# A soft threshold as a relu on ScalarE and one two-step operation on VectorE, in place of a clip and a subtraction on VectorE

## The chip, the cores and the metric

The kernel runs on one core of a Trainium2 chip. The metric is the device time of one execution in microseconds (us), taken as the median of several runs. A core has five engines that work side by side, each through its own instructions in order: TensorE (PE; its weight loads are listed apart as PEld), VectorE (DVE), ScalarE (ACT), GpSimd (POOL) and SyncE (SP), which here issues most of the DMAs. They wait for one another by semaphores.

## The reference: a filter in frequency space, then a gated feed-forward layer

Eight sequences of 3008 rows and 256 channels go through a real Fourier transform along the rows, a complex 256 by 256 product with a bias, a **soft threshold** of the real and of the imaginary part, and the inverse transform. The 24064 rows that come out go through a feed-forward layer with a gate.

```python
X = np.fft.rfft(x, axis=1)
Yr = Xr @ w_r - Xi @ w_i + b_r
Yi = Xr @ w_i + Xi @ w_r + b_i
lam = 0.01
Yr = np.sign(Yr) * np.maximum(np.abs(Yr) - lam, 0.0)
Yi = np.sign(Yi) * np.maximum(np.abs(Yi) - lam, 0.0)
y = np.fft.irfft(Yr + 1j * Yi, n=x.shape[1], axis=1)
...
gate = 1.0 / (1.0 + np.exp(-(x @ w_gate)))
return gate * (x @ w_val) @ w_out
```

The soft threshold draws a value towards zero by 0.01, and values between -0.01 and 0.01 become zero.

## The kernel before

**The transform.** 3008 = 64 x 47, so each transform is two small matrix products with a pass through HBM between them. Stage A (`product_a`, line 186) multiplies along 47, and its result goes to HBM as `zd`. Stage B works for one sequence in 12 steps of `q`, each with two of 24 frequency classes: `fwd_b` multiplies `zf`, read from `zd`, with a table (matmul `pb`, line 247) and splits the result into a rounded high part `xsh` and a rest `xsl` (ScalarE at lines 260 and 264, VectorE at 262 and 265); `mix` is the complex product (matmuls `pm` and `pm3`, line 282), the bias (`yt`, line 284) and the sums `ys` (lines 288 and 289). Then comes `soft`, the soft threshold, from `ys` to `yc`, a tile of 128 partitions by 512 numbers. `mix` splits `yc` into `yh` (ScalarE, line 293) and `yl` (VectorE, line 294), and `inv_b` multiplies these with the inverse table (matmuls `pi`, lines 319 to 321); ScalarE copies the result out of PSUM (`vz`, line 323), and it goes to HBM as `vd`. `inv_a` reads it as `vf` and does the last product (matmul `pia`, line 351), whose result is kept as `yth` and `ytl` or written out as `yf`.

**The feed-forward layer.** The first 9 chunks of 512 rows go through `ffn1` and `ffn2`: matmuls `pg` and `pv` (lines 410 to 412, three for each pair of high and low parts), the sigmoid `sg` (line 416), the product with `pv` (line 418), its split into `hh` and `hl` (lines 426 and 427) and the second product `po` (lines 438 to 440). The rest goes through another form of the same layer, `half`, which holds no soft threshold.

**What sets the order.** The first sequence alone is done in an order written out by hand: steps `q` with `fwd_b(q)`, `mix4(q - 1)` and `inv_b(q - 2)`. `mix4` (line 304 for the matmuls, 306 for the bias) is a form of `mix` that calls `soft` too and hands `yc` on unsplit (line 316). Beside it the weights are unpacked from 64-bit words (`ops`, lines 796 to 804; the relu at 797 takes its bias from the column `ebias`). The other seven sequences run beside the feed-forward chunks. There the loops only give the order of the program, and a scheduler with costs of its own places the instructions on each engine. So a changed operation can move its neighbours. `half` and the last part are again in an order by hand.

**PSUM.** Three banks are shared by `pb`, `pm`, `pm3`, `pi`, `pia` and stage A's `pa` (`FFT_BANKS`), three by `pg` and `pv`, two by `po`. A matmul into a bank waits until ScalarE or VectorE has read what was in it. Each engine takes its instructions in order, so what stands behind a waiting instruction waits as well.

`soft` is called 96 times: 12 times in `mix4` and 84 times in `mix`. The column `ebias` is one of the 128 columns of a tile of which the rest is not used.

Of the kernel before, what the change touches and what calls it, by code (L numbers as in the profile page):

```python
# [9 lines left out]
F32 = mybir.dt.float32  # L10
# [3 lines left out]
AF = mybir.ActivationFunctionType  # L14
ALU = mybir.AluOpType
# [7 lines left out]
LAM = float(np.float32(0.01))  # L23
# [86 lines left out]
def tile_fft_mix_ffn(ctx: ExitStack, tc, x, w_r, w_i, b_r, b_i, w_one, w_out, mf, mi, mis, fa, fb, out):  # L110
    nc = tc.nc

    B, D, S = x.shape[0], w_r.shape[0], R1 * R2
    P = 128
# [12 lines left out]
    sub = nc.vector.tensor_sub  # L127
# [9 lines left out]
    cw = fft.enter_context(tc.tile_pool(name="cw", bufs=1))  # L137
# [8 lines left out]
    def f2k(name):  # L146
        return p2.tile([P, 2, D], F32, tag="f2k", bufs=NF2K, name=name)
# [120 lines left out]

    def soft(s):
        c = f2k("yc")  # L270
        nc.vector.tensor_scalar(c, s, -LAM, LAM, op0=ALU.max, op1=ALU.min)
        sub(c, s, c)
        return c

    def mix(b, q):
        xh, xl = held.pop(("xs", b, q))
        pm = bank("pm")
        p3 = bank("pm3")[:, :D]
        for part, w, o in ((2, 0, pm[:, :D]), (0, 1, pm[:, D:]), (1, 2, p3)):
            mms = [(a[:, ct, part], w_sb[:, ct, v, w]) for ct in range(CT) for a, v in ((xh, 0), (xh, 1), (xl, 0))]  # L280
            for i, (l, r) in enumerate(mms):
                nc.tensor.matmul(o, l, r, start=(i == 0), stop=(i == len(mms) - 1))  # L282
        t = f2k("yt")
        nc.vector.tensor_add(t, pm.rearrange("p (a d) -> p a d", a=2), bias_sb)
        s = f2k("ys")
        for i in range(2):
            rows = slice(64 * i, 64 * i + 64)
            nc.vector.tensor_add(s[0:64, i], p3[rows], t[rows, 0])
            nc.vector.tensor_add(s[64:128, i], t[rows, 0], t[rows, 1])
        c = soft(s)  # L290
        yh = r2k("yh")
        yl = r2k("yl")
        nc.scalar.copy(yh, c)
        sub(yl, c, yh)
        held["ys", b, q] = yh, yl

    def mix4(b, q):
        xh, xl = held.pop(("xs", b, q))
        pm = bank("pm").rearrange("p (q d) -> p q d", q=2)
        for i in range(2):  # L300
            mms = [(a[:, ct, i, at:at + P], w[:, ct, v]) for ct in range(CT)
                   for w, at in ((w_sb[:, :, :, 0], 64), (wi_sb, 0)) for a, v in ((xh, 0), (xh, 1), (xl, 0))]
            for k, (l, r) in enumerate(mms):
                nc.tensor.matmul(pm[:, i], l, r, start=(k == 0), stop=(k == len(mms) - 1))
        s = f2k("ys")
        nc.vector.tensor_add(s, pm, bias4.rearrange("p (o d) -> p o d", o=1).broadcast_to([P, 2, D]))
        held["ys", b, q] = soft(s)
# [444 lines left out]

    bias_sb = cw.tile([P, 2, D], F32, name="bias_sb")
    bias4 = p0.tile([P, D], F32, name="bias4")
    ebias = cw.tile([P, P], F32, name="ebias")[:, :1]
    fb_sb = const.tile([2 * NQ, P], F32, name="fb_sb")
    w1h = const.tile([P, NF, 2, CT, P], F32R, name="w1h")
    w1l = const.tile([P, NF, 2, CT, P], F32R, name="w1l")
# [94 lines left out]
    ffn, own0, u0 = ffn_units()  # L853
    na = R1 // 8
    nc.vector.memset(ebias, -896.0 * 2.0 ** 23)
    mfs, mis_ = {}, {}
    beside = [(b, h) for b in groups[2] for h in range(R1 // 4)]
    waiting = list(beside)
# [142 lines left out]
    for j in range(NF, len(ffn)):  # L1001
        c, f = divmod(j, NF)
# [39 lines left out]
    a, b, c, d = banks[0]  # L1042
# [62 lines left out]
```

## Time and profile before

| | us |
|---|---|
| median of 3 runs | 2779.26 (2777.61 to 2780.85) |
| the profiled execution | 2779.58 |
| its span, from the first instruction's start to the last one's end | 2777.7 |
| TensorE's granted clock over the span | 0.999 of full speed |

The profile's page gives the busy time of each engine, the chain of work that ended last, and the groups of instructions by line, with the mean duration of one and the idle time ahead of them. In the names, `yc<-ys` is an instruction that writes tile `yc` and reads `ys`; `L272` is line 272. The trace can also be asked for the busy time by stretch of time, for a table of who waited for whom, and for a timeline, which gives each instruction's start and length in us, and in brackets how long its engine stood idle before it and what ended that.

### The profile page before, as it was taken

Reading aid. Unit: us, or ns where it says so; the run is one execution under the profiler, and the core shown is the slowest. Engines: PE = TensorE matmul, PEld = TensorE weight load, DVE = VectorE, ACT = ScalarE, POOL = GpSimd, SP = SyncE. Lnnn points to the kernel's source line nnn. Section 1 sums busy time; section 2 is a strip of 40 time slices with the busy share of each in tenths; the row PEclk is TensorE's granted clock in tenths of the full one; section 3 lists DMA queues with packets and bytes.
Section 4 is the critical chain, followed back from the end, with each engine's and each line's share of the span. In section 5 each row is a group of like instructions: output and inputs, shape, how many; then the busy total and the mean of one; then the engine's idle time right before and its main releaser. Section 6 shows DMA issues by size and latency. Waiting matters only on the chain.

```text
span 2777.7 us, 38257 instructions
## 1 busy us (share of the span) xinstructions
PE 2760.4 (99%) x13896; PEld 2305.2 (83%) x13896; DVE 2080.6 (75%) x3109; ACT 1307.4 (47%) x2276; POOL 709.4 (26%) x638
## 2 busy tenths in 40 slices
PE   9999999999999999999999999999999999999999
PEld 6778888888899988888888888888888888888887
DVE  5778778767787636777777777777777777777776
ACT  4665554555455444444444444444444444444443
POOL 0211010223200001333333343333333333333321
PEclk9999999999999999999999999999999999999999
DMA  9867545665554561000000000000000000000000
GB/s 293 266 214 198 171 139 157 193 190 184 178 156 147 168 196 58 31 16 16 31 31 16 16 31 31 31 11 21 31 31 16 16 31 31 27 4 31 31 16 16
DMA packets 173469, 241.01 MB, mean 87 GB/s; under 512 B 14592, under 2 KB 124896, under 8 KB 173280
## 3 DMA queue, kind: packets, MB, share of 16 engines
q1 hardware_dynamic: 163776, 214.93, 25.0%
q0 software_dynamic: 9408, 23.60, 2.6%
q8 instruction: 110, 1.80, 0.3%
q14 instruction: 79, 0.65, 0.1%
q10 hardware_dynamic: 96, 0.04, 0.0%
HBM read 134.17 MB, written 104.33 MB: 86 GB/s over the span
## 4 chain that ended last, share of the span: by engine, by line
PE 95%; DVE 3%; DMA 1%; ACT 1%; issue 0%; SPq 0%; DVEq 0%; ACTq 0%
PE pd L670 11%; PE pc L670 11%; PE pa L670 11%; PE po L646 7%; PE po L645 7%; PE po L647 7%; PE pb L670 6%; PE pm L282 5%; PE pia L351 4%; PE pa L186 3%; PE pb L247 3%; PE pg L410 2%; PE pg L411 2%; PE pg L412 2%; PE pv L410 2%; PE pv L412 2%
## 5 line engine op out<-in xcount | busy, mean ns | idle before, releaser
L647 PE MATMUL po<-hl,w 128*128 128x512 f32 x912 | 354.8, 389 | 0.0
L645 PE MATMUL po<-hh,w 128*128 128x512 f32 x912 | 354.8, 389 | 0.0
L646 PE MATMUL po<-hh,w 128*128 128x512 f32 x912 | 354.8, 389 | 0.0
L729 POOL TENSOR_TENSOR c<-c,c 128x512 f32<-128x512 f32 x114 | 147.7, 1296 | 801.2 <-DVE c L725 588.1
L670 PE MATMUL pc<-s,w1h 128*128 128x512 f32 x912 | 280.8, 389 | 0.0
L670 PE MATMUL pa<-a,w1h 128*128 128x512 f32 x912 | 280.8, 389 | 0.0
L725 DVE TENSOR_TENSOR c<-u,pc 128x512 f32<-128x512 f32 x228 | 156.5, 687 | 91.5 <-PE pc L670 85.6
L700 DVE TENSOR_TENSOR u<-u,pb 128x512 f32<-128x512 f32 x228 | 155.2, 681 | 90.7 <-PE pb L670 61.1
L617 ACT CAST hh<-v 128x512 fp32r<-128x512 f32 x114 | 70.7, 620 | 306.1 <-DVE v L710 306.1
L645 PEld LDWEIGHTS po<-hh,w 128*128 128x128 f32 x912 | 171.2, 188 | 35.6
L670 PEld LDWEIGHTS pc<-s,w1h 128*128 128x128 f32 x912 | 171.2, 188 | 35.5
L670 PEld LDWEIGHTS pa<-a,w1h 128*128 128x128 f32 x912 | 171.2, 188 | 35.5
L647 PEld LDWEIGHTS po<-hl,w 128*128 128x128 f32 x912 | 171.2, 188 | 35.5
L646 PEld LDWEIGHTS po<-hh,w 128*128 128x128 f32 x912 | 171.2, 188 | 35.5
L621 POOL TENSOR_TENSOR hl<-c,hh 128x512 fp32r<-128x512 f32 x114 | 152.3, 1336 | 186.0 <-ACT hh L617 186.0
L282 PE MATMUL pm<-w_sb,xsh 128*128 128x256 f32 x1008 | 188.5, 286 | 1.6 <-ACT xf L187 1.1
L670 PE MATMUL pc<-s,w1l 128*128 128x512 f32 x456 | 177.4, 389 | 0.0
L670 PE MATMUL pa<-a,w1l 128*128 128x512 f32 x456 | 177.4, 389 | 0.0
L702 DVE TENSOR_TENSOR v<-u,pc 128x512 f32<-128x512 f32 x228 | 156.9, 688 | 24.5 <-DVE u L700 0.9
L731 DVE TENSOR_TENSOR u<-u,pd 128x512 f32<-128x512 f32 x228 | 156.6, 687 | 24.5 <-DVE c L725 0.9
L704 DVE TENSOR_TENSOR v<-v,pd 128x512 f32<-128x512 f32 x228 | 156.7, 687 | 24.0 <-DVE v L702 0.5
L696 ACT COPY u<-pa 128x512 f32<-128x512 f32 x228 | 133.7, 586 | 69.4 <-PE pa L670 69.2
(174 smaller groups left out, 6721.1 us busy)
## 6 DMA issues: line engine op xcount, KB each, us to landing
zf<-zd SPq DMA_DIRECT2D x96, 256.0 KB, 3.6
vf<-vd SPq DMA_DIRECT2D x128, 192.0 KB, 3.0
out_dram<-ot SPq DMA_DIRECT2D x93, 256.0 KB, 2.2
vd<-vz SPq DMA_DIRECT2D x84, 256.0 KB, 2.8
ypair<-yd SPq DMA_DIRECT2D x19, 1024.0 KB, 4.9
yd<-yf SPq DMA_DIRECT2D x103, 188.0 KB, 2.9
xf<-in_x_dram SPq DMA_DIRECT2D x48, 384.0 KB, 4.1
zd<-xf SPq DMA_DIRECT2D x44, 384.0 KB, 3.3
```

What stands on the lines that cost most here:

```text
L282: nc.tensor.matmul(o, l, r, start=(i == 0), stop=(i == len(mms) - 1))
L621: sub_(hl, h, hh)
L645: nc.tensor.matmul(o, wh, hh, start=(f == 0), stop=False)
L646: nc.tensor.matmul(o, wl, hh, start=False, stop=False)
L647: nc.tensor.matmul(o, wh, hl, start=False, stop=(f == NF - 1))
L670: nc.tensor.matmul(o, l, r, start=not more and l is wh and r is xh, stop=l is wl, skip_group_check=more)
L700: add(u, u, b)
L702: add(v, u, c)
L704: add(v, v, d)
L725: add(c12, u, c)
L729: nc.gpsimd.tensor_mul(c12, g12, c12)
L731: add(u, u, d)
```

## The change

In `soft`, the clip to the band from -0.01 to 0.01 and the subtraction of the clipped value give way to two other operations. With s the input and LAM = 0.01, ScalarE computes c = relu(s - LAM), and VectorE then computes min(s + LAM, c) in one operation of two steps. Above the band that is s - LAM, below it s + LAM, and zero within. ScalarE's activation takes its bias from a tile, so a second column of the tile of `ebias` is filled with -LAM.

```diff
     def soft(s):
         c = f2k("yc")
-        nc.vector.tensor_scalar(c, s, -LAM, LAM, op0=ALU.max, op1=ALU.min)
-        sub(c, s, c)
+        nc.scalar.activation(c, s, AF.Relu, bias=lam_sb)
+        nc.vector.scalar_tensor_tensor(c, s, LAM, c, op0=ALU.add, op1=ALU.min)
         return c
...
-    ebias = cw.tile([P, P], F32, name="ebias")[:, :1]
+    both = cw.tile([P, P], F32, name="ebias")
+    ebias, lam_sb = both[:, :1], both[:, 1:2]
...
     nc.vector.memset(ebias, -896.0 * 2.0 ** 23)
+    nc.vector.memset(lam_sb, -LAM)
```

Lines 271 and 272 keep their numbers: 271 is now ScalarE's relu and 272 VectorE's two-step operation. Lines behind 755 move on by one, those behind 857 by two.

**Place 1, the first sequence, in the order by hand.** ScalarE's queue in one step of `q`: the end of a weight's unpacking (`w_107`, `raw`), then the copy `vz` out of PSUM and the parts `xsh` and `xsl` of the next step. Before:

```order
L803 CAST w_107<-raw_297 128x2x256
L800 ACTIVATE raw_408<-raw_408 128x512
L323 COPY vz<-pi 128x512
L253 CAST xsh<-pb 128x4x128
L256 ACTIVATE xsh<-xsh 128x4x64
L256 ACTIVATE xsl<-xsl 128x4x64
```

And with the change:

```order
L804 CAST w_107<-raw_298 128x2x256
L801 ACTIVATE raw_409<-raw_409 128x512
L271 ACTIVATE yc<-ys,ebias 128x512
L323 COPY vz<-pi 128x512
L253 CAST xsh<-pb 128x4x128
L256 ACTIVATE xsh<-xsh 128x4x64
L256 ACTIVATE xsl<-xsl 128x4x64
```

The relu, which waits for `ys` from VectorE, stands ahead of `vz`, `xsh` and `xsl`. (Its bias is listed under the name of the tile, `ebias`.) Nothing else moves; on VectorE one operation stands where two stood.

**Place 2, the fourth soft threshold of the second sequence, where the scheduler sets the order.** VectorE's queue before, with the last two sums into `ys` first, then the sum `xsf` and the rest `xsl` for the next step, the rest `yl`, and the next step's `yt`:

```order
L288 TENSOR_TENSOR ys<-pm_2138,yt 64x256
L289 TENSOR_TENSOR ys<-yt 64x256
L262 TENSOR_TENSOR xsf<-xsf 128x2x128
L271 TENSOR_SCALAR yc<-ys 128x512
L272 TENSOR_TENSOR yc<-ys,yc 128x512
L265 TENSOR_TENSOR xsl<-xsf,xsh 128x768
L294 TENSOR_TENSOR yl<-yc,yh 128x512
L284 TENSOR_TENSOR yt<-pm,bias_sb 128x512
```

And with the change:

```order
L288 TENSOR_TENSOR ys<-pm_2139,yt 64x256
L289 TENSOR_TENSOR ys<-yt 64x256
L262 TENSOR_TENSOR xsf<-xsf 128x2x128
L284 TENSOR_TENSOR yt<-pm,bias_sb 128x512
L272 SCALAR_TENSOR_TENSOR yc<-ys,yc 128x512
L265 TENSOR_TENSOR xsl<-xsf,xsh 128x768
L294 TENSOR_TENSOR yl<-yc,yh 128x512
```

The next step's `yt` has moved ahead of the threshold. TensorE's queue at the same place, matmuls of `pg` and `pv` around the first ones that read `yh` and `yl`, before:

```order
L412 MATMUL pg<-yth,w1l 128x512
L319 MATMUL pi<-yh,mi_sb 128x256
L410 MATMUL pg<-yth,w1h 128x512
L411 MATMUL pg<-ytl,w1h 128x512
L412 MATMUL pg<-yth,w1l 128x512
L410 MATMUL pv<-yth,w1h 128x512
L320 MATMUL pi<-yl,mi_sb 128x256
```

And with the change:

```order
L412 MATMUL pg<-yth,w1l 128x512
L410 MATMUL pg<-yth,w1h 128x512
L411 MATMUL pg<-ytl,w1h 128x512
L412 MATMUL pg<-yth,w1l 128x512
L410 MATMUL pv<-yth,w1h 128x512
L319 MATMUL pi<-yh,mi_sb 128x256
L411 MATMUL pv<-ytl,w1h 128x512
L412 MATMUL pv<-yth,w1l 128x512
L410 MATMUL pv<-yth,w1h 128x512
L320 MATMUL pi<-yl,mi_sb 128x256
```

L319, which reads `yh`, now stands behind four more matmuls. Over the whole program TensorE's instructions are the same, and their order differs at a score of places like this one. In 72 of the 96 units of the change, VectorE's two-step operation stands directly behind the last sum into `ys`; in the other 24, one or two operations of another step lie between. SP's loads and stores change places with a neighbour at about thirty places.

## The prediction

> **What bounds the kernel now.** I read the page first, for the shares and the chain of work that ended last.
>
> ```profile
> span 2777.7 us, 38257 instructions
> PE 2760.4 (99%) x13896; PEld 2305.2 (83%) x13896; DVE 2080.6 (75%) x3109; ACT 1307.4 (47%) x2276; POOL 709.4 (26%) x638
> PE 95%; DVE 3%; DMA 1%; ACT 1%; issue 0%; SPq 0%; DVEq 0%; ACTq 0%
> ```
>
> TensorE is busy for 2760.4 of 2777.7 us and holds 95% of the chain. All its idle time together is 17.3 us. Next the table by stage says where the touched lines lie: the soft threshold runs 12 times between 35 and 95 us and 84 times between 190 and 950 us, and nowhere else.
>
> ```profile
> 35.00:95.00 60.00, 56.62 (x419) 52.83 (x418) 48.83 (x86) 34.63 (x66) 8.96 (x13) 0.97 0.90 277
> 190.00:430.00 240.00, 237.66 (x1463) 202.17 (x1462) 191.41 (x342) 122.22 (x204) 28.80 (x42) 1.00 0.57 168
> 430.00:690.00 260.00, 259.20 (x1601) 220.69 (x1600) 189.46 (x321) 131.22 (x225) 52.35 (x82) 1.00 0.60 183
> 690.00:950.00 260.00, 258.82 (x1775) 236.91 (x1774) 202.29 (x356) 130.38 (x224) 19.62 (x29) 1.00 0.51 153
> 1065.00:2778.00 1713.00, 1708.51 (x7537) 1414.44 (x7535) 1336.23 (x1825) 770.50 (x1345) 571.57 (x426) 1.00 0.07 23
> ```
>
> The columns are the stretch, then the busy time of TensorE, weight loads, VectorE, ScalarE and GpSimd. From 190 to 950 us TensorE is busy for 237.66 + 259.20 + 258.82 = 755.7 of 760 us: 4.3 us idle. VectorE is busy for 583 us (77%), ScalarE for 384 (50%). The 1713 us behind 1065 hold no soft threshold. The change does not touch a matmul, so it can act only through the waits of TensorE. These are they, from the tables of who waited for whom between 190 and 950 us (us in total, times, longest):
>
> ```profile
> PEld pa L186 <- ACT vz L323: 7.2, 11, 0.7
> PEld pia L351 <- DVE ys L288: 4.9, 5, 1.4
> PEld pi L319 <- ACT yh L293: 2.4, 5, 0.7
> PEld pa L186 <- ACT yf L367: 1.5, 5, 0.3
> PEld pa L186 <- ACT hh L426: 1.1, 4, 0.3
> PEld pi L320 <- DVE yl L294: 0.2, 1, 0.2
> PE pi L319 <- ACT yh L293: 0.6, 2, 0.3
> ```
>
> PEld is the weight load, which runs ahead of the matmul, so its wait need not stop TensorE. The soft threshold's own product, yh and yl, is waited for 6 times in 84, for 2.6 us of weight loads and 0.6 us of matmul.
>
> **The two operations.** Lines of the groups by shape, with total busy time and the mean of one:
>
> ```profile
> L271 DVE TENSOR_SCALAR yc<-ys 128x512 f32<-128x512 f32 x96 | 43.3, 451 | 2.8
> L272 DVE TENSOR_TENSOR yc<-ys,yc 128x512 f32<-128x512 f32 x96 | 67.7, 705 | 2.8
> L783 DVE SCALAR_TENSOR_TENSOR wn<-wf 128x512 f32<-128x512 f32 x1 | 0.7, 680 | 0.0
> L798 DVE SCALAR_TENSOR_TENSOR cv_e<-raw,cv_e 128x512 uint32<-128x512 uint32 x18 | 12.4, 688 | 1.2 <-ACT cv_e L797 1.2
> L797 ACT ACTIVATE cv_e<-cv_e,ebias 128x512 int32<-128x512 int32 x18 | 13.0, 722 | 15.1 <-DVE cv_e L796 15.1
> L707 ACT ACTIVATE v<-v 128x512 f32<-128x512 f32 x114 | 72.0, 632 | 105.8 <-DVE v L704 105.8
> L187 ACT ACT_TABLE_LOAD x1 | 1.3, 1283 | 5.1 <-DMA xf<-in_x_dram 5.1
> L416 ACT ACT_TABLE_LOAD x1 | 1.3, 1283 | 0.0
> ```
>
> Removed on VectorE: 0.451 + 0.705 = 1.156 us a unit, 96 x 1.156 = 111 us. Added there: one operation in two steps, which the trace has in the same size at 0.680 and 0.688 us; I take 0.69, or 66 us in all. Its busy time falls by 45 us. Added on ScalarE: a relu from SBUF to SBUF with its bias in a tile. L797 is a relu of that size with such a bias (0.722, on whole numbers), and L707 an activation without one (0.632). I take 0.722, the nearer row; 96 x 0.722 = 69 us. L797 runs 18 times among sigmoids and copies with two table loads in the whole run, so a relu brings no load. The new memset of one column costs about what its neighbour does, under 0.1 us while the inputs are on their way: nothing.
>
> The Trainium skill speaks against one term: "Vector Engine (DVE) Microarchitecture Reference", section "Points that are easy to get wrong", says that the operation in two steps runs at half throughput when both sources lie in SBUF and are not bf16. An estimate from that page would be about 512 x 2 cycles, 1.07 us, and the saving on VectorE would shrink from 45 to about 8 us. The trace disagrees: L783 has two f32 sources in SBUF and took 0.680 us.
>
> **Busy time is not what VectorE's queue sees.** In the order of the change, the two-step operation stands directly behind the last sum into ys in 72 of the 96 units. There VectorE waits while ScalarE does the relu. Before, a unit held its queue for 0.451 + 0.035 + 0.705 = 1.19 us (0.03 us is the step between two instructions in the timelines below, on one engine and across two alike); now for 0.03 + 0.722 + 0.03 + 0.69 = 1.47 us. So the path from ys to yc grows by 0.28 us, and VectorE gets its 0.47 us back only in the other 24 units. ScalarE has room: between 190 and 950 us it stood idle before yh, waiting for yc:
>
> ```profile
> ACT yh L293 <- DVE yc L272: 44.9, 60, 2.1
> ```
>
> That is 0.75 us at each of 60 units, into which a relu of 0.722 fits.
>
> **Place 1, 35 to 95 us** (timeline; start, length):
>
> ```profile
> 62.81 0.69 ACT L800 ACTIVATE raw<-raw 128x512 f32<-128x512 uint32 x1
> 63.37 0.68 DVE L306 TENSOR_TENSOR ys<-pm,bias 128x512 f32<-128x512 f32 x1
> 64.00 0.59 ACT L323 COPY vz<-pi 128x512 f32<-128x512 f32 x1 [0.50 <-PE pi L316]
> 64.54 0.69 DVE L272 TENSOR_TENSOR yc<-ys,yc 128x512 f32<-128x512 f32 x1
> 66.23 0.42 ACT L256 ACTIVATE xsl<-xsl 128x256 fp32r<-128x256 f32 x1 [0.31 <-DVE xsl L254]
> 67.42 1.02 PE L316 MATMUL pi<-yc,mi_sb 128*128 128x256 f32 x4
> 69.09 0.48 PE L304 MATMUL pm<-w_sb,xsh 128*128 128x256 f32 x2
> ```
>
> The relu stands ahead of vz, xsh and xsl on ScalarE. ScalarE is free at 63.50, ys ends at 64.05, the relu then runs 64.08 to 64.80, the two-step operation until 65.52; it was 65.23. TensorE wants yc at 67.42: 1.9 us are left. Behind the relu vz ends about 65.4 instead of 64.59, and xsl about 67.2 instead of 66.65; TensorE wants xsl from 69.09, behind xsh. Nothing is late, so these 12 units cost nothing. Without that cover it would be 12 x 0.28 = 3.4 us.
>
> **Place 2, 190 to 950 us, a unit without slack:**
>
> ```profile
> 218.83 0.42 DVE L289 TENSOR_TENSOR ys<-yt 64x256 f32<-64x256 f32 x1
> 219.28 0.43 DVE L262 TENSOR_TENSOR xsf<-xsf 128x256 f32<-128x256 f32 x1
> 220.08 0.69 DVE L272 TENSOR_TENSOR yc<-ys,yc 128x512 f32<-128x512 f32 x1
> 220.32 0.40 PE L410 MATMUL pg<-yth,w1h 128*128 128x512 f32 x1
> 220.56 0.40 PE L411 MATMUL pg<-ytl,w1h 128*128 128x512 f32 x1
> 220.80 0.62 ACT L293 CAST yh<-yc 128x512 fp32r<-128x512 f32 x1 [0.23 <-DVE yc L272]
> 221.48 0.39 PE L319 MATMUL pi<-yh,mi_sb 128*128 128x256 f32 x1 [0.28 <-ACT yh L293]
> ```
>
> TensorE stood for 0.28 us until yh ended. In the change's order four matmuls of L410 to L412 now go ahead of L319; at the step of 0.24 us between the two rows above that is 0.95 us, so L319 would be due at 221.48 - 0.28 + 0.95 = 222.15. On VectorE the operation yt (L284, about 0.69) moves ahead of the two-step one: 219.71 + 0.03 + 0.69 + 0.03 = 220.46, then 0.69 and 0.62 with their steps give yh at about 221.85. L319 is no longer kept waiting. Most of the other 78 units keep microseconds: the 6 waits above are all there are.
>
> **The sum**, against the profiled execution's own 2779.58 us (2777.7 of span and 1.9 around it; the median of the runs is 2779.26): at worst six waits longer by 0.28, +1.7 us; at best the 3.2 us of waits for yh and yl gone. I take +0.7 us for a few relus that come at a bad moment: **2780 us**, no change that shows. About 0.2%, or 5.6 us, is what a measurement can tell from none.
>
> **Rivals.** (1) **ScalarE's queue becomes the bound**, slower. A relu waits for ys, and what evacuates PSUM behind it (vz, yf, xf, xsf) comes late by up to 0.75 us. Weight loads already waited for vz, yf and hh 20 times. All of them later by 0.75 would be 15 us; half, with TensorE's queue covering the rest, some 8 us: 2788. It decides where ScalarE is still in the relu when a bank is due. For it: those 20 waits, and TensorE short of only 4.3 us. Against: ScalarE at 50%, and the idle 44.9 us. The Trainium skill, "ScalarE: Activation LUTs", section "Rules for kernel authors", would put relu, max and min on VectorE and not on ScalarE; by that rule this change goes the wrong way, as in this rival. The rows bear the rule out for one operation (0.722 against 0.451 us), not for the time. (2) **VectorE's relief reaches TensorE**, faster: the 4.9 us for ys, the 3.2 for yh and yl go: 2779.6 - 8.1 = 2771.5. For it: VectorE is busier than ScalarE (77%). Against: in 72 units its queue is held longer, not shorter. (3) A reordered load or store lands late, as SP's order moves by a few places: 2 to 4 us, 2783.
>
> **How the numbers follow.** Forecast 0.62, rival 3 0.08, rival 1 0.20, rival 2 0.10. The range goes from 2773, most of the way to rival 2, to 2789, past rival 1: about 0.85 of the chance. Within 0.2% are the forecast and rival 3, so faster 0.10, same 0.70, slower 0.20.
>
> **What would show it.** The relu's mean near 0.72 and the two-step operation's near 0.69; VectorE's busy time down by some 45 us, ScalarE's up by some 69; TensorE's idle time between 190 and 950 us still about 4 us, with waits for yh, vz and ys of the same size. Waits for vz or xsf that have doubled speak for rival 1, waits for ys that are gone for rival 2. A relu with a table load beside each, or TensorE idle for tens of us, would make all of it wrong.

## The result and the profile after

| | before | after |
|---|---|---|
| median, us | 2777.60 (22 runs, 2775.57 to 2780.85) | 2779.79 (22 runs, 2777.86 to 2796.70) |
| the profiled execution, us | 2779.58 | 2778.75 |
| its span, us | 2777.7 | 2776.6 |

The ratio of after to before is 1.0018, with an interval of 1.001 to 1.0025: slower, clear of 1, and about the 0.2% that the prediction took for the least that shows. That is also the ratio of the means. The medians are only 2.2 us apart (0.08%), and after's is 0.2 us from the forecast. What the medians hide is the upper end: 6 of the 22 runs of after took between 2787.61 and 2796.70 us, and none of before's took over 2780.85. Those six runs are the part of the result that the prediction did not have, and most of the experiments are about them.

The page of after, its span, busy times and chain:

```profile
span 2776.6 us, 38244 instructions
PE 2760.6 (99%) x13896; PEld 2305.7 (83%) x13896; DVE 2040.3 (73%) x3014; ACT 1366.0 (49%) x2372; POOL 709.7 (26%) x638
PE 95%; DVE 2%; ACT 1%; DMA 1%; issue 0%; POOL 0%; SPq 0%; DVEq 0%; ACTq 0%
```

VectorE's busy time fell by 40.3 us and ScalarE's rose by 58.6, and TensorE stands where it stood. The groups by shape, for the two new operations (count, then total and mean; behind the bar the idle time ahead of them):

```profile
L271 ACT ACTIVATE yc<-ys,ebias 128x512 f32<-128x512 f32 x96 | 69.4, 723 | 58.2 <-DVE ys L289 52.1 <-DVE ys L306 5.5
L272 DVE SCALAR_TENSOR_TENSOR yc<-ys,yc 128x512 f32<-128x512 f32 x96 | 67.6, 704 | 59.4 <-ACT yc L271 58.4
```

The relu takes 0.723 us, the two-step operation 0.704. The idle columns show the new handover: ScalarE stands still for ys, then VectorE for the relu. The busy times by stage between 190 and 950 us, columns as in the prediction:

```profile
190.00:430.00 240.00, 238.05 (x1470) 203.09 (x1469) 182.17 (x314) 141.07 (x233) 29.93 (x42) 1.00 0.57 168
430.00:690.00 260.00, 259.72 (x1609) 221.59 (x1608) 177.54 (x296) 147.75 (x252) 51.80 (x80) 1.00 0.60 183
690.00:950.00 260.00, 258.52 (x1768) 236.38 (x1767) 188.88 (x326) 147.76 (x253) 20.01 (x31) 1.00 0.51 153
```

Who waited there for whom (us in total, times, longest), weight loads, then ScalarE and VectorE:

```profile
PEld pa L186 <- ACT vz L323: 7.2, 11, 0.7
PEld pia L351 <- DVE ys L288: 5.2, 5, 1.8
PEld pm L282 <- DVE ys L288: 1.3, 1, 1.3
PEld pi L319 <- ACT yh L293: 0.4, 2, 0.2
...
ACT yc L271 <- DVE ys L289: 52.1, 65, 2.3
ACT yh L293 <- DVE yc L272: 19.7, 48, 0.8
...
DVE yc L272 <- ACT yc L271: 48.8, 60, 1.0
```

TensorE is busy for 238.05 + 259.72 + 258.52 = 756.3 of 760 us, so it is idle for 3.7 us there, against 4.3. The waits for vz are the same 7.2 us in 11 places. VectorE now loses 48.8 us to the relus, 0.81 us at each of 60 units, more than the 40 us of work it was relieved of, and TensorE's idle time there does not grow. The 84 units of `mix` cost nothing that this profile shows.

The first sequence is another matter. This is its end, the hand-over of units 10 and 11 (the twelve counted from 0) and the start of stage A behind them, from the timeline of before, VectorE, ScalarE and TensorE (start, length; in brackets the idle time ahead and what ended it):

```profile
88.92 1.02 PE L316 MATMUL pi<-yc,mi_sb 128*128 128x256 f32 x4
89.15 0.68 DVE L306 TENSOR_TENSOR ys<-pm,bias 128x512 f32<-128x512 f32 x1
89.99 0.58 ACT L323 COPY vz<-pi 128x512 f32<-128x512 f32 x1 [0.61 <-PE pi L316]
91.50 1.03 PE L316 MATMUL pi<-yc,mi_sb 128*128 128x256 f32 x4
93.34 0.67 PE L186 MATMUL pa<-xf,fa_sb 94*96 94x512 f32 x1 [0.81 <-DVE xf L187]
```

And the same place in after:

```profile
88.25 0.71 ACT L271 ACTIVATE yc<-ys,ebias 128x512 f32<-128x512 f32 x1
...
90.11 1.02 PE L316 MATMUL pi<-yc,mi_sb 128*128 128x256 f32 x4
...
90.97 2.13 PE L186 MATMUL pa<-xf,fa_sb 94*96 94x512 f32 x4
91.26 0.68 DVE L306 TENSOR_TENSOR ys<-pm,bias 128x512 f32<-128x512 f32 x1
91.98 0.72 ACT L271 ACTIVATE yc<-ys,ebias 128x512 f32<-128x512 f32 x1 [0.50 <-DVE ys L306]
...
92.61 0.56 ACT L323 COPY vz<-pi 128x512 f32<-128x512 f32 x1
92.73 0.69 DVE L272 SCALAR_TENSOR_TENSOR yc<-ys,yc 128x512 f32<-128x512 f32 x1 [0.79 <-ACT yc L271]
...
93.53 1.10 PE L316 MATMUL pi<-yc,mi_sb 128*128 128x256 f32 x4 [0.43 <-ACT vz L323]
...
95.74 0.67 PE L186 MATMUL pa<-xf,fa_sb 94*96 94x512 f32 x1 [1.12 <-DVE xf L187]
```

Follow vz, the copy of unit 10's inverse product out of PSUM. Before, ScalarE began it at 89.99, 1.07 us behind the product's start. Now it stands in ScalarE's queue behind unit 11's relu, which waits for ys, and begins at 92.61, 2.50 us behind. The next product (unit 11) needs that bank, and TensorE stands for 0.43 us. Then it stands for 1.12 us until VectorE has copied a result of stage A out of PSUM (`xf`, line 187), where it was 0.81. The idle time is small, 1.55 us in all against 0.81. What it can bring shows in the experiments.

### The profile page after: what moved, and what is told of

Read it like the earlier page. It is cut to its first block, busy times and chain, and to the rows that moved or that the text cites. A ratio compares the mean times of both kernels' runs of the same rounds, so it can differ in the third digit from the quotient of the medians.

```text
span 2776.6 us, 38244 instructions
## 1 busy us (share of the span) xinstructions
PE 2760.6 (99%) x13896; PEld 2305.7 (83%) x13896; DVE 2040.3 (73%) x3014; ACT 1366.0 (49%) x2372; POOL 709.7 (26%) x638
## 4 chain that ended last, share of the span: by engine, by line
PE 95%; DVE 2%; ACT 1%; DMA 1%; issue 0%; POOL 0%; SPq 0%; DVEq 0%; ACTq 0%
PE pd L670 11%; PE pc L670 11%; PE pa L670 11%; PE po L647 7%; PE po L646 7%; PE po L645 7%; PE pm L282 6%; PE pb L670 6%; PE pia L351 4%; PE pa L186 3%; PE pb L247 3%; PE pg L410 2%; PE pg L412 2%; PE pg L411 2%; PE po L438 2%; PE pv L410 2%
## 5 line engine op out<-in xcount | busy, mean ns | idle before, releaser
L282 PE MATMUL pm<-w_sb,xsh 128*128 128x256 f32 x1008 | 188.5, 286 | 1.9 <-DVE ys L288 1.1
```

## The experiments

The expectations weigh theories by letter. M is that the units have slack, which hides the longer path; A is that ScalarE's queue is the bound; L is that the end of the first sequence brings the long runs, by the last unit alone, and L2 by the last two. S is that something that starts or lands a little earlier or later tips some executions over, and S2 that all twelve relus of the first sequence share in it. The first run is the changed kernel unaltered; the others change the lines given. In all of them `soft_old` is the clip and the subtraction of before:

```diff
+    def soft_old(s):
+        c = f2k("yc")
+        nc.vector.tensor_scalar(c, s, -LAM, LAM, op0=ALU.max, op1=ALU.min)
+        sub(c, s, c)
+        return c
```

All results together. "Long" counts the runs over 2787 us; every one of them has a mean granted clock of 0.992 to 0.996, and no other run in the first eleven rows is below 0.997. (One run of before has 0.949 on record at 2780.59 us, so a low mean clock alone does not make a long run.) Before, on the same chips, took 2778.10 us in the median of 111 runs, the longest of them 2781.76. Four single runs of 3048 to 8429 us, two of them of before, one of warm and one of relu3, are left out of this table.

| run | what has the new threshold | median, us (runs) | ratio to before | long |
|---|---|---|---|---|
| after | all 96 | 2779.79 (22) | 1.0018 [1.001, 1.0025] | 6 |
| again | all 96 | 2779.69 (11) | 1.0008 [0.9999, 1.0017] | 2 |
| first_only | the 12 of `mix4` | 2781.05 (12) | 1.0014 [1.0005, 1.0022] | 2 |
| rest_only | the 84 of `mix` | 2778.92 (11) | 1.0002 [0.9994, 1.0011] | 0 |
| last_old | all but the last of the 12 | 2779.27 (11) | 1.0002 [0.9993, 1.001] | 0 |
| warm | all, and six useless matmuls | 2779.94 (11) | 1.0004 [0.9995, 1.0012] | 0 |
| last_only | the last of the 12 | 2778.86 (11) | 1.0003 [0.9994, 1.0011] | 0 |
| last_two | the last two of the 12 | 2779.16 (11) | 1.0005 [0.9996, 1.0014] | 0 |
| vz_late | none; one more pass ahead of vz | 2779.55 (11) | 1.0004 [0.9995, 1.0012] | 0 |
| vz_late3 | none; three more passes ahead of vz | 2778.66 (11) | 1.0004 [0.9995, 1.0013] | 0 |
| relu_dve | all 96, both steps on VectorE | 2779.36 (11) | 1.0004 [0.9996, 1.0013] | 0 |
| relu3 | all 96, the relu three times | 2815.27 (3) | 1.0132 [1.0117, 1.0146] | – |
| relu3_rest | the 84, the relu three times | 2788.59 (5) | 1.0035 [1.0022, 1.0047] | – |

### Which units: again, first_only, rest_only

```diff
 # first_only: in mix
-        c = soft(s)
+        c = soft_old(s)
 # rest_only: in mix4
-        held["ys", b, q] = soft(s)
+        held["ys", b, q] = soft_old(s)
```

For again:

> The changed kernel once more, to see whether its runs again lie 2 us over those of before (2779.79 against 2777.60 in the median) and again scatter upwards (8 of 22 runs above 2782, up to 2796.7; none of 22 before). Theory M (TensorE alone is the bound, the soft threshold is off the path, what is left is scatter): ratio 1.000 to 1.001, few runs above 2782. Rival A (ScalarE's queue makes TensorE's banks late): ratio 1.0015 to 1.003 with a steady shift of 4 to 8 us, and TensorE idle longer between 190 and 950 us. Rival S (something that starts or lands at a slightly different time tips some executions over): most runs within 1 us of before, a third of them 4 to 18 us over.

For first_only:

> Relu and two-step operation only in the 12 units of the first sequence; the 84 others as before. TensorE's, SP's and POOL's order is that of before throughout. M: ratio 1.000, 2777.6. A: 1.000 too, since its 84 units are as before. S, if it is the opening, where DMA is at nine tenths: the scatter upwards as in the changed kernel.

For rest_only:

> Relu and two-step operation only in the 84 units between 190 and 950 us; the 12 of the first sequence as before. TensorE's and SP's order is that of the changed kernel. M: ratio 1.000 to 1.001. A: the whole shift, as in the changed kernel. S, if it is the order of loads and stores behind 190 us: the scatter as in the changed kernel; if it is the opening: none.

The unaltered kernel gave 1.0008 this time, and two long runs of 11. The 84 units alone give 1.0002 with no long run, in the order of instructions that the change brings there: neither the longer path nor the reordering costs anything that 11 runs can tell from nothing (the interval ends at 1.0011). The 12 units alone give 1.0014 with two long runs of 12. So what the change costs, as far as these runs can tell, it costs in the twelve units.

Three kernels have long runs, 10 of 45 or 22% together. At that rate a kernel with 11 runs shows none in about 6% of cases by chance (0.78 to the power of 11). So one zero in the table says little by itself. The eight kernels without a long run have 88 runs together, and before has 111.

The profiled executions of again and first_only were themselves long ones (spans of 2790.4 and 2789.4 us). The busy times by stretch of again (stretch, then TensorE, weight loads, VectorE, ScalarE and GpSimd, the granted clock, DMA):

```profile
93.05:96.46 3.41, 1.86 (x7) 0.92 (x6) 2.73 (x5) 1.46 (x4) 0.72 (x1) 1.00 0.29 106
96.46:123.77 27.31, 26.69 (x59) 15.28 (x58) 8.67 (x15) 10.14 (x18) 4.49 (x8) 0.50 0.64 197
```

The granted clock is at half for 27.31 us just behind the two gaps of TensorE. Work at half clock for 27.31 us loses 13.7; the span is 13.8 longer than that of after (2790.4 - 2776.6). That is the whole of this long run. (The six of after lie 8 to 17 us above its median, so they are not all of one size.) In first_only the same happens at 95.20 us.

### How far the slack goes: relu3, relu3_rest

The relu is done three times, and ScalarE's part of each unit grows by 2 x 0.723 = 1.45 us; in relu3_rest `mix4` has `soft_old` as well.

```diff
-        nc.scalar.activation(c, s, AF.Relu, bias=lam_sb)
+        for _ in range(3):
+            nc.scalar.activation(c, s, AF.Relu, bias=lam_sb)
```

> The relu three times in a row into the same tile, in all 96 units: two more of 0.72 us on ScalarE and on the path from ys to yc, 1.45 us a unit, 139 us of ScalarE in all. M: the path has microseconds of slack in nearly all units, so at most +5 us (ratio up to 1.002). A: three times the price of one relu or more; if one costs 2 to 5 us, this is 7 to 20 us over before (1.003 to 1.007). S: no steady shift, scatter as its order of DMAs happens to fall.

> The relu three times in a row in the 84 units between 190 and 950 us, the 12 of the first sequence as before; to see how much of the 38 us of three relus everywhere belongs to the 84. M (the path from ys to yc has slack there): 0 to 6 us over before, ratio up to 1.002; the other 32 us or more belong to the first sequence and to the halved clock behind it. Rival A (ScalarE's queue is the bound in the 84 units): 15 us or more, ratio 1.005 or more.

relu3 took 37 us more than before, far more than slack allows, and M's figure failed. relu3_rest took 10 us more, between M's figure and that of A. By difference the other 27 us belong to the first sequence. The busy times by stretch of relu3:

```profile
50.00:110.00 60.00, 46.35 (x316) 40.22 (x316) 34.43 (x59) 45.71 (x79) 7.28 (x10) 0.99 0.63 195
109.17:129.65 20.48, 19.92 (x34) 8.57 (x33) 7.95 (x14) 7.28 (x13) 4.76 (x9) 0.50 0.68 213
```

The waits of TensorE in it from 35 to 110 us, and the stretch of after to compare with:

```profile
PE pm L305 <- DVE ys L307: 7.5, 6, 1.6
PE pi L317 <- ACT vz L324: 1.9, 1, 1.9
```

```profile
50.00:110.00 60.00, 57.54 (x374) 47.55 (x374) 42.81 (x72) 39.65 (x76) 11.75 (x18) 1.00 0.85 261
```

In relu3 TensorE is idle for 13.65 of the 60 us, in after for 2.46; that is 11.2 us, with ys and vz waited for. Then it runs at half clock for 20.48 us, which loses 10.2. Together they are 21 of the 27 us; the other 6 stay open. In the 84 units of relu3_rest the path from ys to yc is 0.28 + 1.45 = 1.73 us longer than in before, and that costs 10.35 / 84 = 0.12 us each. Not all of it is waiting: the profile of relu3_rest has two stretches of 3.41 us at half clock, at 697.98 and 1008.60 us, which lose 1.7 us each. The units have slack for the 0.28 us of the change, not without end: the waits of relu3_rest between 190 and 950 us begin with

```profile
PE pia L358 <- DVE yt L291: 2.1, 5, 0.6
PE pi L326 <- ACT xsf L260: 1.1, 1, 1.1
```

which after does not have at that size. So waits of the kind of rival 1 do come with a long enough ScalarE part, and the change stays below the point from which they decide.

### Is it the engine: relu_dve

Both operations go to VectorE, in the place of the old ones.

```diff
-        nc.scalar.activation(c, s, AF.Relu, bias=lam_sb)
+        nc.vector.tensor_scalar(c, s, -LAM, 0.0, op0=ALU.add, op1=ALU.max)
```

> Both operations on VectorE in all 96 units: relu of s minus 0.01 as a tensor-scalar operation, then the two-step one. TensorE's, ScalarE's, SP's and POOL's order is that of before, VectorE's too but for the operation's kind. It tells the engine from the operation: if the two-step operation costs what the subtraction did (0.69 to 0.71 us), ratio 0.9995 to 1.0005, no wait for vz, no run 8 us over before. If the two-step operation is at half throughput (1.07 us): VectorE 34 us busier, ratio 1.001 or more.

Its two groups by shape:

```profile
L272 DVE SCALAR_TENSOR_TENSOR yc<-ys,yc 128x512 f32<-128x512 f32 x96 | 67.7, 706 | 2.8
L271 DVE TENSOR_SCALAR yc<-ys 128x512 f32<-128x512 f32 x96 | 43.4, 452 | 2.8
```

The ratio is 1.0004, with no long run. The two-step operation costs what the subtraction did (0.706 us for 0.705), and the other step 0.452 for 0.451: without the move to ScalarE the new form costs what the old one did. That the long runs need the move fits its 11 runs without one, which alone would not show it.

### Where the clock falls: last_old, warm, last_only, vz_late

L said that the wait for vz at the last unit is enough. Two of these were to take it away from after, and two to put it into before:

```diff
 # last_old: after, in mix4
+        held["ys", b, q] = soft_old(s) if q == NP - 1 else soft(s)
 # last_only: before, in mix4
+        held["ys", b, q] = soft(s) if q == NP - 1 else soft_old(s)
 # vz_late: before, behind the threshold in mix4
+        if q == NP - 1:
+            nc.scalar.activation(p0.tile([P, 2, D], F32, name="scratch"), s, AF.Relu, bias=lam_sb)
 # warm: after, ahead of and behind the last inverse product
+                keep_warm(bank("warm", "l1", L1_BANKS), wf[:, 0, :P], wf, 2)
...
+                keep_warm(bank("warm", "l1", L1_BANKS), wf[:, 0, :P], wf, 4)
```

> The changed kernel with the clip and the subtraction put back in that one unit alone. L: the wait for vz is gone and the one for xf is back at 0.8 us, ratio 0.999 to 1.0005, no run 8 us over before. S2: as the changed kernel, ratio 1.001 to 1.002, a quarter of the runs 8 us over.

> The changed kernel with six matmuls of no use (128 by 512, 0.23 us each) into a bank of their own at the end of the first sequence: two ahead of the last inverse product, where TensorE waited 0.43 us, four behind it, where it waited 1.1 us. The sums of the program are as they were. L, if TensorE's idleness there is what lets the clock fall: no run 8 us over before, median within 1 us of before. If the clock falls for another reason: the scatter stays as in the changed kernel.

> The kernel before with the relu and the two-step operation in one unit alone, the twelfth and last of the first sequence; every other instruction stands where it stood in before. Theory L (the price lies at the end of the first sequence: the copy vz of the unit before stands behind this relu, TensorE waits for the PSUM bank and, behind it, for the copies of stage A; now and then the granted clock then falls to half for some 27 us): TensorE waits 0.3 to 0.5 us for vz and 1.0 to 1.2 us for xf near 94 us; median 0.5 to 2 us over before, and 2 to 5 of 11 runs 8 us or more over it. Rival S2 (all twelve relus share the price, by a ScalarE queue that is longer in each step): a twelfth of it, nothing to be seen, no run 8 us over before.

> The kernel before with one more ScalarE pass over ys, into a tile that nothing reads, in the last unit of the first sequence, just ahead of vz; the threshold itself is as before in all 96 units. It costs 0.72 us of ScalarE once, and yc is not later. L, if vz behind ScalarE is the cause: TensorE's wait for vz as in last_only, and the halved clock in some runs. If it is the longer path from ys to yc instead: no wait for vz, as before.

Taking it away worked: neither last_old nor warm has a wait for vz or a long run, in 11 runs each. Two figures of the expectations failed there: the wait for xf stays at 1.13 us in last_old and does not go back to 0.8, and the median of warm is 1.8 us above before's, not within 1. Putting it in did not work: last_only and vz_late do not wait for vz at all and have no long run either, so these two kernels do not test the wait, and L's forecast for a single unit failed. The wait of warm for xf shows what the six useless matmuls do:

```profile
PE pa L186 <- DVE xf L187: 0.2, 1, 0.2
```

Of 1.55 us of idle time 0.2 is left.

### Two units, or a longer wait: last_two, vz_late3

```diff
 # last_two: before, in mix4
+        held["ys", b, q] = soft(s) if q >= NP - 2 else soft_old(s)
 # vz_late3: before, behind the threshold in mix4
+        if q == NP - 1:
+            scratch = p0.tile([P, 2, D], F32, name="scratch")
+            for _ in range(3):
+                nc.scalar.activation(scratch, s, AF.Relu, bias=lam_sb)
```

> The kernel before with the relu and the two-step operation in the last two units of the first sequence, the eleventh and the twelfth; all else stands as in before. Theory L2 (two relus in a row at the end add up: the first holds up the unpacking on ScalarE and VectorE, so the last ys comes late, its relu too, and vz behind it; TensorE waits for vz, and only then may the clock fall): a wait for vz of about 0.4 us near 93 us, as in the changed kernel, and 1 to 4 of 11 runs 8 us or more over before. Rival S2 (it takes all twelve): no wait for vz, no such run.

> The kernel before with three more ScalarE passes over ys, into a tile that nothing reads, just ahead of vz in the last unit of the first sequence; the threshold is as before in all 96 units. vz comes about 2 us later, TensorE should wait for it by 0.5 to 1 us. L2, if idleness of TensorE at this place is what lets the clock fall: 1 to 4 of 11 runs 8 us or more over before, though no threshold has changed. If the new threshold itself is needed: median up by 0.5 to 1 us and no such run.

last_two has no wait for vz and no long run, so L2 failed as well, and what S2 said of this run came out. Its timeline says why (here L277 is the relu, L322 the inverse product and L329 vz):

```profile
84.00 0.71 ACT L277 ACTIVATE yc<-ys,ebias 128x512 f32<-128x512 f32 x1
86.48 1.02 PE L322 MATMUL pi<-yc,mi_sb 128*128 128x256 f32 x4
87.34 1.88 PE L186 MATMUL pa<-xf,fa_sb 94*96 94x512 f32 x4
88.36 0.56 ACT L329 COPY vz<-pi 128x512 f32<-128x512 f32 x1
89.28 1.10 PE L322 MATMUL pi<-yc,mi_sb 128*128 128x256 f32 x4
91.49 1.10 PE L186 MATMUL pa<-xf,fa_sb 94*96 94x512 f32 x2 [1.11 <-DVE xf L187]
```

From unit 10's relu to vz ScalarE takes 88.36 - 84.00 = 4.36 us, and in after 92.61 - 88.25 = 4.36 us: the same. But unit 10's product starts 2.48 us behind that relu, and in after 1.86 us. TensorE lies 0.62 us closer behind ScalarE once all twelve units have the new threshold, and so finds the bank full. By the two timelines the wait needs both: ScalarE's order in the last units, and a lead that the ten units ahead have used up. No run sets that lead by itself.

vz_late3 makes TensorE wait for longer at that place, and has no long run in 11:

```profile
92.82 1.13 PE L326 MATMUL pi<-yc,mi_sb 128*128 128x256 f32 x4 [0.96 <-ACT vz L333]
```

The wait for vz is 0.96 us, but none for xf follows it. So this wait as such does not bring long runs at the rate of after, unless chance hid them.

### What decides, read from the profiles

The half-clock stretches of the profiled executions are 3.41, 20.48 and 27.31 us long: 1, 6 and 8 times 3.41. A halving as such is nothing new: nine stretches of one step stand in seven of the profiles, one of them in before, at 39.38 us, and at half clock such a step loses 1.7 us. What is new in again, first_only and relu3 is the length. Where the clock changes several times in one execution, all the changes lie whole multiples of that step apart. In again the two changes of clock lie on a grid of that step (96.46 + 8 x 3.414 = 123.77), and so a stretch of 3.41 us ahead of 96.46 can be looked at by itself, as above: TensorE was busy for 1.86 of it. These are the two gaps in it, from TensorE's timeline:

```profile
93.65 1.10 PE L316 MATMUL pi<-yc,mi_sb 128*128 128x256 f32 x4 [0.43 <-ACT vz L323]
95.86 1.48 PE L186 MATMUL pa<-xf,fa_sb 94*96 94x512 f32 x2 [1.12 <-DVE xf L187]
```

First_only has the same:

```profile
91.79:95.20 3.41, 1.86 (x6) 0.92 (x6) 2.84 (x5) 1.46 (x4) 0.73 (x1) 1.00 0.26 93
95.20:122.51 27.31, 26.69 (x58) 15.14 (x57) 8.68 (x15) 10.36 (x19) 4.50 (x8) 0.50 0.64 197
```

In after the only half-clock stretch of that length, at 35.84 us, gives the grid (35.84 + 16 x 3.414 = 90.46):

```profile
35.84:39.26 3.42, 3.42 (x19) 3.42 (x18) 1.03 (x2) 2.06 (x4) 0.00 (x0) 0.50 1.03 384
90.47:93.88 3.41, 2.98 (x10) 1.17 (x9) 2.62 (x5) 1.90 (x3) 0.41 (x1) 1.00 0.62 205
93.88:97.29 3.41, 2.29 (x8) 1.05 (x7) 1.77 (x4) 2.17 (x5) 1.00 (x3) 1.00 0.22 77
```

In first_only and again both gaps, 0.43 and 1.12 us, fall into one step, which leaves 1.86 us of work, and the clock halves at its end. In after the border at 93.88 lies between them, the steps hold 2.98 and 2.29 us of work, and the clock stays. The profile of after thus holds the same idle time as that of again and is 13.8 us shorter.

This reading also gives how often it should happen. From the start of the first gap to the end of the second it is 95.86 - 93.22 = 2.64 us in again (starts 93.65 and 95.86, gaps 0.43 and 1.12); both lie in one step of 3.41 us where the grid falls well, in (3.41 - 2.64) / 3.41 = 23% of the cases. Measured: 10 long runs in the 45 of after, again and first_only, 22%. That the two agree so closely is partly luck, since a count of 10 in 45 fits any rate from about 13 to 36%. And there are none in the kernels that lack one of the gaps: with 1.1 us alone (last_only, last_two, last_old) or 0.96 alone (vz_late3) the step of 3.41 us around the gap holds 2.18 us of work (last_old) or more. At this place the least work with which the clock stayed is 1.99 us, in relu3 from 102.35 to 105.76 us; the step behind that one holds 1.48 us, and at its end the clock halves.

The length is another question. All three long stretches begin just ahead of, or in, a row of 18 matmuls of stage A (in again it lasts from 95.86 to 111.00 us), and they end 3 us (relu3) to 13 us (again) behind its last one; in the nine short ones `pm` or `pg` matmuls follow. That the matmuls of stage A hold the clock down is a guess from where they stand, and no run tests it.

The reading was found behind the runs, from these profiles and a count, and no run set the grid's place on purpose. So it is well supported that the cause lies in the two gaps, and how they halve the clock is not shown. Nor is idle time in a step the whole rule; two steps, of again and of last_only, speak against that. The first:

```profile
31.61:35.02 3.41, 1.80 (x14) 1.67 (x15) 0.61 (x1) 1.00 (x2) 0.00 (x0) 1.00 0.77 207
35.02:38.43 3.41, 3.28 (x29) 3.08 (x27) 0.91 (x3) 1.80 (x4) 0.00 (x0) 1.00 0.93 289
```

The second:

```profile
102.96:106.37 3.41, 2.54 (x19) 2.10 (x18) 0.99 (x2) 1.01 (x3) 0.00 (x0) 1.00 1.00 354
106.37:109.78 3.41, 3.41 (x8) 2.73 (x9) 1.30 (x3) 1.64 (x2) 0.00 (x0) 0.50 1.04 359
```

In again 1.80 us of work kept the clock, in last_only 2.54 did not. What kind of matmul fills a step may count; no run tests it.

## Why the prediction held, and where it did not

- **The bound.** TensorE is busy for 2760.6 us before and after to 0.2 us, and holds 95% of the chain. The forecast of no visible change rests on that, and in the median it came out: 2779.79 us for 2780. That it is within 0.2 us is luck. The forecast added 0.7 us to one execution's 2779.58; the median of before in 22 runs is 2777.60, so the change was 2.2 us, three times the term. And a median says nothing of the long runs, which the forecast did not have.
- **The prices.** The relu was put at 0.722 us and took 0.723; the two-step operation at 0.69 and took 0.704. VectorE should lose 45 us: by rows it is 43.3 + 67.7 - 67.6 = 43.4, and 40.3 in the busy total. ScalarE should gain 69: by its row it is 69.4, in the busy total 58.6. The sum of all ScalarE rows rises by 68.7, so the difference is overlap, which the busy total counts once (vz begins at 92.61 where the relu runs until 92.70).
- **The page's price** of about 1.07 us for the two-step operation, by the Trainium skill, "Vector Engine (DVE) Microarchitecture Reference", section "Points that are easy to get wrong", does not hold here: 96 of them with two f32 sources in SBUF took 0.704 us in the mean, as long as the subtraction (0.705), which has two sources as well. The price took that operation's rate as the one that is halved, and that sentence of the Trainium skill does not say which rate it means: against the clip, with one source and 0.451 us, the two-step operation is slower here.
- **VectorE's queue** was to be held for 1.47 us in a unit. At unit 11 it is 93.42 - 91.94 = 1.48 us from the end of ys to that of the two-step operation.
- **Place 2 and the 84 units.** At place 2 L319 starts without a wait, as worked out. All waits of weight loads for yh went from 2.4 us to 0.4, where the list of signs had them of the same size. The change in the 84 units alone gives 1.0002. This is shown by rest_only, and its limit by relu3_rest.
- **Place 1: here a step failed.** "Nothing is late, so these 12 units cost nothing" was worked out on a step in the middle, at 63 to 69 us, and carried to all twelve. At the last one the working would have gone otherwise: unit 11's relu stands ahead of vz there and waits for ys, and the product that needs vz's bank is the next thing that TensorE has to do. The price worked out for lost cover, 12 x 0.28 = 3.4 us, was of the wrong kind as well. The idle time at that place grew by only 0.7 us, but in again and first_only 27.31 us at half clock followed it. In 33 runs of after and again the mean is 2782.3 us, 4.1 above before's 2778.2: 8 long runs by some 12 us give 2.9 of these. The other 1.2 us, and the 2.1 us by which the ten other runs of first_only lie above before in the mean, are not explained beyond those 0.7.
- **Rival 1** (ScalarE's queue as the bound) is not there in the 84 units, where the waits for vz are 7.2 us in 11 places as before. Its mechanism, vz late behind a relu, is the one that acts at the end of the first sequence, at one place and not at 20.
- **Rival 2** (VectorE's relief reaches TensorE): the waits for ys went from 4.9 to 5.2 us, with 1.3 more at L282, and not away. relu_dve gives VectorE its full work back, and takes no longer.
- **Rival 3** (reordered transfers): rest_only has the new order where the order changed, at 1.0002.

No version here beats before: the intervals of rest_only, last_old and relu_dve include 1, and these are what to take if the form of the change is wanted and no long run in 11 is enough.

## What to carry to other kernels

With one engine busy for 99% of the span, moving work between two others was worth nothing here, and its cost lay at a seam: check a hand-over at the last step of a loop, where the next work has no cover, and not at a middle one. When the median hardly moves, look at every run's time and granted clock before calling it no change; here a group of runs some 12 us up had a mechanism behind it, and it began with less than 2 us of idle time. To see how far slack goes, triple the added cost in one part of the program and not in all of it.

## What the runs showed of the hardware

- A clock fall can last long: in again and first_only TensorE ran at half clock for 27.31 us, though it was busy for 26.69 of them. In relu3 it was 20.48 us; in nine other places, one in before, it was one step of 3.41.
- The lengths agree with the Trainium skill, "TensorE: Matmul & The Clock Gate", section "What's actually happening", which has a free-running window of 3413 ns and a result that differs from run to run. By its table the clock halves behind an idle window and comes back behind a busy one. The stretches of one step agree with the coming back: the clock of after returned at 39.26 us behind a step with 3.42 us of work. In again it halved behind a window with 1.86 us of work in 3.41, and took eight windows to come back, of which TensorE was busy for 26.69 us: there the measurement goes against the table on both points, and no run here shows why.
- A relu on ScalarE handed to VectorE costs no more between the engines than a result handed on within VectorE: in after it is 0.03 us from the relu's end (91.98 + 0.72 = 92.70) to the two-step operation's start (92.73), and in before 0.03 us from the clip's end (89.87 + 0.43 = 90.30) to the subtraction's start (90.33).
